# Rounds of maxima in twos on four PSUM banks, ahead of the main loop of a fused attention and MLP kernel

## The chip, the cores and the metric

The kernel runs on one core of a Trainium2 chip. The time is that of one execution on the device, in microseconds; three executions of the kernel before took 2324.1, 2325.55 and 2324.93 us, median 2324.93.

## The reference

For x of 2048 tokens by 576 channels the kernel computes `g * a + (1 - g) * b`:

```
g = sigmoid((x * gate_w).sum(-1))
a = softmax(q k^T * 18**-0.5) v, 32 heads of 18, then @ wo        (q, k, v = x @ wqkv)
b = gelu(layernorm(x) @ w1 + b1) @ w2 + b2                        (576 -> 4608 -> 576)
```

All of it is float32. The kernel splits each operand of a projection into a rounded high part and the rest, a low part, and multiplies high by high, high by low and low by high.

## The kernel before

**Two stages.** The first works through four blocks of 512 tokens (`tb` 0 to 3). For each block it transposes x on TensorE (`x_chunk`, five pieces, L711), copies the high parts with ScalarE and subtracts for the low parts with VectorE, and then does 17 groups (`g` 0 to 16): nine `qk_group`s (L784 to L787, 14 matmuls of 128 rows and 512 columns each, results copied and subtracted in L790 and L791, both stored to HBM) and eight `v_group`s (L805 to L808, 14 matmuls of 288 columns; copied by ScalarE in L812 or VectorE in L814, stored to `v_scr` after every second one). In between stand the layer norm of the block on VectorE (`norm`, L753 to L773), the transposes of the next block's x (after groups 2 to 6) and of the normed x (`y_chunk`, L735 and L736, stored to `y_scr`, after groups 8 to 12, in block 0 after 11 to 15).

The second stage is a loop of 512 steps: 32 units (a pair of heads by half of the queries), 16 blocks of keys each. It interleaves scores and exponentials of one unit (L250, L253), the weighted sum over v (L268), the maxima of the next unit (L210, L212) and, as filler of TensorE, the MLP (L460, L538).

**Rounds of maxima.** Softmax needs each row's maximum before the exponentials. A round (`s1_round`) is two matmuls of 54 rows, one for each head of the pair, in the upper and the lower half of the array (L210), into a PSUM bank each, and two VectorE reductions (L212). A unit has 32 rounds; the loop does two in a step. Since the loop starts with unit 0's exponentials, all 32 rounds of unit 0 and eight of unit 1 are done ahead of it. The table `ROUNDS` says after which groups of which block a round is put: one after each group from 8 on in block 1, from 2 on in block 2, from 5 on in block 3, 36 in all. The last four stand alone between the blocks and the loop (L1089, each with a call of `run_due`).

**PSUM.** Its eight banks in the first stage: four in the pool `ps_a` for the projections, three in `ps_s1` for all transposes and all rounds, and one in `ps_o`, which is first used by the loop. A pool's banks are handed out in turn, and the next user of a bank waits until the last one has been read. `score_bank` gives a round its banks.

**Order of the work.** Each engine does its instructions in the order in which the program writes them. SyncE's queue issues nearly all transfers, in order too, and an issue that waits for its data holds up those behind it. Small tasks are put at fixed places by `run_due`, which counts slots: one after each group of block 2 from group 4 on, one after each group of block 3 up to group 8 and two after each later one, then about four to a step of the loop. The first weights of the MLP are read ahead of the loop: `load_w1` and `load_w2` issue the reads of raw weights into buffers (one for w1, two for w2) and enter in `LOADED` the slot from which a `split` may use them: 5 and 3 slots later, in the loop 8 and 6. The split copies the high part with ScalarE (L370), subtracts on GpSimd (L166) and then lets the next raw piece be read into the buffer (L349, L355). Splits are first entered in block 3's group 9; a model of GpSimd's queue spreads them.

The weights of the first stage come in seven pieces (`W_CUT`); `split_w` copies the high part with ScalarE (L705) and subtracts on VectorE for pieces 0 and 1, on GpSimd for the others (L706). A group's matmuls wait for the pieces that they read.

Of the kernel before, what the change touches and what calls it, by code (L numbers as in the profile page):

```python
# [36 lines left out]
NS1 = 3  # L37
# [3 lines left out]
LAND = 8  # L41
# [5 lines left out]
LAST = 28  # L47
PSTEP = (489, 494, 497, 499)
ORDER = (0, 1, 3, 2)
ROUNDS = [lambda g: 0, lambda g: int(g >= 8), lambda g: int(g >= 2), lambda g: int(g >= 5)]  # L50
SLOTS = [lambda g: 0, lambda g: 0, lambda g: int(g >= 4), lambda g: 1 if g < 9 else 2]
SKIP = 0
N_AT = 5
# [7 lines left out]
def gated_mix_kernel(ctx: ExitStack, tc: tile.TileContext, x, wqkv, wo, w1, b1, w2, b2, gate_w, out):  # L61
    nc = tc.nc
# [32 lines left out]
    ps_s1 = ctx.enter_context(tc.tile_pool(name="ps_s1", bufs=NS1, space=PSUM))  # L95
    ps_o = ctx.enter_context(tc.tile_pool(name="ps_o", bufs=1, space=PSUM))
# [4 lines left out]
    def psum(pool):  # L101
        return pool.tile([P, TB], F32, name="ps")

    ring = [0]

    def score_bank():

        if not looped[0]:
            return psum(ps_s1)
        ring[0] += 1  # L110
        return psum(ps_s1 if ring[0] % (NS1 + 2) < NS1 else ps_s2)

    def big_tile():
# [5 lines left out]
    def bcast_rows(ap, n):  # L119
        return bass.AP(tensor=ap.tensor, offset=ap.offset, ap=[[0, P], [1, n]])  # L120
# [6 lines left out]
    slot = [0]  # L127
# [183 lines left out]
    looped = [False]  # L311

    def next_round():
        if rounds:
            u, r = rounds.pop()
            s1_round(u, r)
            if r == NR - 1:
                defer(1, lambda: s1_finish(u))


    def mlp():
# [3 lines left out]
        n = len(seq)  # L325
# [3 lines left out]
        def chunk(q):  # L329

            i, m = divmod(q, G // 2)
            return i, m, seq[i][1] * G + 2 * m
# [5 lines left out]
        LOADED = {}  # L338
        NQ0 = npair // NB

        def load_w1(q):

            if (1, q) in LOADED or q >= NQ0:
                return
            LOADED[1, q] = slot[0] + (LAND if looped[0] else 5)
            fc = chunk(q)[2]
            for h in range(2):
                src = w1[:, (fc + h) * P:(fc + h + 1) * P]
                nc.sync.dma_start(R1[64 * h:64 * h + 64], src.rearrange("(c p) n -> p c n", p=64))  # L349

        def load_w2(c):
            if (2, c) in LOADED or c >= NFC:
                return
            LOADED[2, c] = slot[0] + (LAND - 2 if looped[0] else 3)
            nc.sync.dma_start(R2[c % 2], w2[c * P:(c + 1) * P, :])  # L355

        def rounded(dst, src):
# [254 lines left out]
        for i in range(n + 1):  # L612
            q = 2 * i
# [49 lines left out]
    with ExitStack() as a:  # L663
        wpool = a.enter_context(tc.tile_pool(name="a_w", bufs=1, side="right"))
        sm = a.enter_context(tc.tile_pool(name="a_sm", bufs=2, side="right"))
        ps_a = a.enter_context(tc.tile_pool(name="ps_a", bufs=4, space=PSUM))
# [11 lines left out]
        def x_view(tb):  # L678
            return xt[tb].rearrange("p (t d) -> p t d", d=D + 64)
# [12 lines left out]
        def load_w(n):  # L692
            cs = slice(W_CUT[n], W_CUT[n + 1])
            wide = W_CUT[n + 1] - W_CUT[n]
            raw = pp.tile([P, 2, 2, TB], F32, name="p").rearrange("p a b c -> p (a b c)")[:, :5 * wide]
            raw = wraw[n] = raw.rearrange("p (c n) -> p c n", n=wide)
            nc.sync.dma_start(raw[:, 0:4, :], wqkv[0:512, cs].rearrange("(c p) n -> p c n", p=P))
            nc.sync.dma_start(raw[0:64, 4, :], wqkv[512:576, cs])
            nc.sync.dma_start(raw[64:128, 4, :], wqkv[512:576, cs])

        def split_w(n, eng):
            c0 = W_CUT[n] if W_CUT[n] < 2 * D else W_CUT[n] - 2 * D
            hi, lo = [w_[:, :, c0:c0 + W_CUT[n + 1] - W_CUT[n]] for w_ in (W_QK if W_CUT[n] < 2 * D else W_V)]
            raw = wraw.pop(n)
            nc.scalar.activation(hi, raw, AF.Copy)  # L705
            eng.tensor_tensor(lo, raw, hi.bitcast(F32), op=ALU.subtract)  # L706

        def transposed(tb, c):
            ps = psum(ps_s1)
            for t in range(4):  # L710
                nc.tensor.transpose(ps[:, t * P:(t + 1) * P], x_view(tb)[:, t, c * P:(c + 1) * P], ident)  # L711
            return ps
# [3 lines left out]
        def x_chunk(tb, c):  # L716

            if c == 0:
                xT[tb] = big_tile()
            big = xT[tb]  # L720
            ps = transposed(tb, c)
            if c < 4:
                nc.scalar.activation(big[:, c, :], ps, AF.Copy)
                nc.vector.tensor_tensor(big[:, 4 + c, :], ps, big[:, c, :].bitcast(F32), op=ALU.subtract)
            else:
                tmp = hp.tile([P, TB], F32R, name="hh")
                nc.scalar.activation(tmp, ps, AF.Copy)
                nc.scalar.activation(big[0:64, 8, :], ps[0:64], AF.Copy)
                nc.vector.tensor_tensor(big[64:128, 8, :], ps[64:128], tmp[64:128, :].bitcast(F32), op=ALU.subtract)

        def y_chunk(tb, c):
            ps = transposed(tb, c)
            eh = hp.tile([P, TB], F32R, name="hh")
            el = hp.tile([P, TB], F32R, name="hl")
            nc.scalar.activation(eh, ps, AF.Copy)  # L735
            nc.vector.tensor_tensor(el, ps, eh.bitcast(F32), op=ALU.subtract)  # L736
            for s_, e in enumerate((eh, el)):
                if c < 4:
                    nc.sync.dma_start(y_scr[tb, s_, 2 * c:2 * c + 2].rearrange("c p n -> (c p) n"), e.bitcast(F32))
                else:  # L740
                    nc.sync.dma_start(y_scr[tb, s_, 8], e[0:64].bitcast(F32))
# [94 lines left out]
        for tb in range(NB):  # L836
            work = [(qk_group, (tb, mt)) for mt in (range(9) if tb < 2 else (4, 0, 1, 2, 3, 5, 6, 7, 8))] + [(v_group, (tb, t, n)) for t in range(4) for n in range(2)]
            for g, (fn, args) in enumerate(work):
                if tb == 0:
                    if g in W_AT:  # L840
                        n = W_AT[g]
                        split_w(n, nc.gpsimd if n > 1 else nc.vector)
                        if n + 2 < 7:
                            load_w(n + 2)
                    if g == 10:
                        nc.sync.dma_start(b2b, bcast_rows(b2, D))
                        nc.sync.dma_start(b1r, b1.rearrange("(c p) -> c p", p=P))
                if tb == NB - 1 and g == 16:
                    args += (lambda: next(stream[0]),)
                fn(*args)  # L850
                ng = g - (N_AT if tb == 0 else 2)
                if 0 <= ng < 4:
                    norm(tb, ng)
                if tb + 1 < NB and 2 <= g < 7:
                    x_chunk(tb + 1, g - 2)
                yg = g - (11 if tb == 0 else 8)
                if 0 <= yg < 5:
                    y_chunk(tb, yg)
                if g == (16 if tb == 0 else 13) and tb + 2 < NB:
                    load_x(tb + 2)  # L860
                if tb == NB - 1:
                    if g == 1:
                        load_k(0, 3 * TB, S)
                    if g == 2:
                        load_q(1)
                        next(stream[0])
                    if g == 9:
                        qkstack.close()
                        wp1 = mstack.enter_context(tc.tile_pool(name="m_w1", bufs=3))
                        wp2 = mstack.enter_context(tc.tile_pool(name="m_w2", bufs=4))  # L870
                        next(stream[0])

                        nc.scalar.activation(gate, glog, AF.Exp, scale=-1.0)
                    if g == 14:
                        nc.vector.tensor_scalar(gate, gate, 1.0, None, op0=ALU.add)
                        nc.vector.reciprocal(gate, gate)
                        nc.vector.tensor_scalar(gate1, gate, -1.0, 1.0, op0=ALU.mult, op1=ALU.add)
                    if g == 7:
                        ps = psum(ps_s1)
                        nc.tensor.transpose(ps[:, :NFC], b1r, ident[:NFC, :NFC])  # L880
                        nc.vector.tensor_copy(b1t, ps[:, :NFC])
                if tb == 1 and g == 5:
                    load_q(0)
                    load_k(0, 0, TB)
                if tb == 1 and g == 9:
                    load_k(0, TB, 2 * TB)
                if tb == 2 and g == 4:
                    load_k(0, 2 * TB, 3 * TB)
                for _ in range(ROUNDS[tb](g)):
                    next_round()  # L890
                for _ in range(SLOTS[tb](g)):
                    run_due()
# [282 lines left out]
```

## Time and profile before

| | |
|---|---|
| median of three executions | 2324.93 us |
| profiled execution | 2325.55 us |
| its span, first to last instruction | 2323.8 us |
| mean granted TensorE clock | 0.996 |
| first loop matmul (L250) starts | 250.09 us into the span |
| rounds' reductions (L212), mean | 685 ns |

The span is one execution, recorded by the hardware profiler. In the lines below, a timeline row gives start and length in us, engine, line, operation, output and inputs, shapes, the number of instructions that were merged, and in brackets the idle time just before with what ended it. PE is TensorE's matmuls, PEld its weight loads, DVE is VectorE, ACT ScalarE, POOL GpSimd, SPq SyncE's queue. A matmul's length includes its way through the array, so the distance between starts tells the pace. Rows of stretches give the busy time of each engine, the granted clock and the DMA engines' mean share.

### The profile page before, as it was taken

The numbers are of one execution on the slowest core, as the hardware profiler recorded it, in microseconds if no ns is written. First come the engines' busy times: TensorE is split into PE (matmuls) and PEld (weight loads), VectorE is DVE, ScalarE is ACT, GpSimd is POOL, SyncE is SP. The second block draws the span as 40 slices with busy tenths as digits, with TensorE's granted clock in tenths as the row PEclk, the third lists the DMA queues.
The fourth block names the chain that finished last, engine by engine and source line by source line (L and its number), as shares of the span: only waits on it lengthen the run. The fifth ranks groups of instructions, "written<-read, shape, count | busy, mean of one in ns | idle before, by whom it ended". The sixth has DMA issues, their size and how long they took to land.

```text
span 2323.8 us, 51438 instructions
## 1 busy us (share of the span) xinstructions
PE 2292.7 (99%) x20585; PEld 1544.4 (66%) x20585; DVE 1664.8 (72%) x2890; ACT 1441.9 (62%) x2773; POOL 967.7 (42%) x965
## 2 busy tenths in 40 slices
PE   8998999999999999999999999999999999999999
PEld 7876666666666666666666666666666666666658
DVE  5665677777777777777777777777777777777734
ACT  4222577777776666666676666666666666666662
POOL 4001466666564433333353444444434333333700
PEclk9999899999999999999999999999999999999999
DMA  7747855444456524243263424242364233242264
GB/s 245 244 149 232 232 171 147 149 140 146 137 190 167 159 96 118 99 138 111 77 172 136 157 96 130 88 136 96 118 162 152 96 111 107 97 146 96 77 210 161
DMA packets 165022, 330.31 MB, mean 142 GB/s; under 512 B 57190, under 2 KB 84490, under 8 KB 154054
## 3 DMA queue, kind: packets, MB, share of 16 engines
q1 hardware_dynamic: 163162, 323.76, 44.3%
q8 instruction: 162, 2.65, 0.5%
q10 hardware_dynamic: 1620, 3.26, 0.4%
q14 instruction: 78, 0.64, 0.1%
HBM read 234.16 MB, written 96.58 MB: 142 GB/s over the span
## 4 chain that ended last, share of the span: by engine, by line
PE 92%; DVE 3%; DMA 2%; ACT 1%; issue 1%; SPq 1%; POOL 0%; ACTq 0%; DVEq 0%; POOLq 0%
PE ps L268 20%; PE ps L538 20%; PE ps L460 20%; PE ps L250 13%; PE ps L210 12%; PE ps L1071 3%; PE ps L784 3%; PE ps L805 2%; DVE m L212 1%; DMA qk_scr<-hh 1%; DMA p<-in_A_wqkv_dram 0%; PE ps L711 0%; ACT p L253 0%; DMA x<-in_B_w_dram 0%; DVE x L773 0%
## 5 line engine op out<-in xcount | busy, mean ns | idle before, releaser
L212 DVE TENSOR_REDUCE m<-ps 128x1 f32<-128x512 f32 x2048 | 1314.8, 685 | 393.7 <-PE ps L210 372.2
L253 ACT ACTIVATE p<-ps 128x512 f32<-128x512 f32 x1368 | 740.6, 594 | 372.2 <-PE ps L250 361.9
L166 POOL TENSOR_SCALAR zz<-zz 128x512 f32<-128x512 f32 x288 | 178.6, 620 | 819.1 <-ACT zz L513 802.9
L460 PE MATMUL ps<-big,w 64*128 64x512 f32 x3888 | 510.4, 393 | 0.1
L253 ACT ACTIVATE ring<-ps 128x512 f32<-128x512 f32 x680 | 368.2, 594 | 187.6 <-PE ps L250 182.9
L538 PE MATMUL ps<-w,hh 64*128 64x288 f32 x4352 | 466.3, 299 | 4.0 <-ACT token L547 3.5
L210 PE MATMUL ps<-ka,qa 54*128 54x512 f32 x2048 | 457.9, 422 | 11.0 <-DVE hl L736 6.5
L250 PE MATMUL ps<-qa,ka 56*128 56x512 f32 x2048 | 454.7, 423 | 0.7 <-DVE m L212 0.4
L460 PEld LDWEIGHTS ps<-big,w 64*128 64x128 f32 x3888 | 371.4, 185 | 82.3 <-ACT z L481 0.4
L538 PEld LDWEIGHTS ps<-w,hh 64*128 64x128 f32 x4352 | 370.7, 186 | 45.5 <-ACT token L547 17.3
L166 POOL TENSOR_TENSOR zz<-zz,z 128x512 f32<-128x512 f32 x288 | 371.7, 1291 | 24.0
L250 PEld LDWEIGHTS ps<-qa,ka 56*128 56x128 f32 x2048 | 204.3, 184 | 216.6 <-DVE m L212 180.8
L268 PE MATMUL ps<-p,vt 128*32 128x512 f32 x2736 | 345.0, 599 | 0.0
L538 PE MATMUL ps<-w,hl 64*128 64x288 f32 x2176 | 333.8, 293 | 0.0
L210 PEld LDWEIGHTS ps<-ka,qa 54*128 54x128 f32 x2048 | 206.6, 186 | 110.6 <-ACT p L253 42.4
L166 POOL TENSOR_TENSOR w<-x,w 128x576 fp32r<-128x576 f32 (+1 forms) x54 | 98.3, 1836 | 307.2 <-DMA qk_scr<-hh 172.2
L538 PEld LDWEIGHTS ps<-w,hl 64*128 64x128 f32 x2176 | 215.5, 185 | 0.3 <-POOL hl L166 0.3
L166 POOL TENSOR_TENSOR hl<-zz,hh 128x512 fp32r<-128x512 f32 x136 | 176.6, 1299 | 11.3
L268 PE MATMUL ps<-ring,vt 128*32 128x512 f32 x1360 | 179.1, 598 | 0.0
L268 PEld LDWEIGHTS ps<-p,vt 128*32 128x32 f32 x2736 | 71.5, 109 | 161.2 <-issue 153.9
L556 DVE SCALAR_TENSOR_TENSOR x<-ps,x 128x288 f32<-128x288 f32 x256 | 105.1, 452 | 57.3 <-PE ps L538 57.3
L784 PE MATMUL ps<-big,wqk 128*128 128x512 f32 x432 | 109.7, 402 | 1.5 <-POOL wqk L706 1.4
(101 smaller groups left out, 1394.0 us busy)
## 6 DMA issues: line engine op xcount, KB each, us to landing
w<-w_scr SPq DMA_DIRECT2D x54, 1152.0 KB
w<-w_scr SPq DMA_DIRECT2D x108, 576.0 KB
x<-in_B_w_dram SPq DMA_DIRECT2D x72, 288.0 KB
w_scr<-w SPq DMA_DIRECT2D x18, 1152.0 KB
w_scr<-w SPq DMA_DIRECT2D x36, 576.0 KB
big<-y_scr SPq DMA_DIRECT2D x42, 384.0 KB
qa<-qk_scr SPq DMA_DIRECT2D x192, 72.0 KB
ka<-qk_scr SPq DMA_DIRECT2D x84, 144.0 KB
```

The lines of the kernel that those rows point to most:

```text
L166: fn(*args, **kw)
L210: nc.tensor.matmul(ps, qa[r0:r0 + 54, t * P:(t + 1) * P], ka[r0:r0 + 54, kb * TB:(kb + 1) * TB], start=True, stop=True)
L212: nc.vector.tensor_reduce(M4[u][:, h, t, kb:kb + 1], ps, axis=AX.X, op=ALU.max)
L250: nc.tensor.matmul(ps[h], ka[r0:r0 + 56, kc * P:(kc + 1) * P], qa[r0:r0 + 56, qb * TB:(qb + 1) * TB], start=True, stop=True)
L253: nc.scalar.activation(RING[n % 3][:, qb, h], ps[h], AF.Exp, scale=SCALE)
L268: nc.tensor.matmul(OB[u][r:r + 32, :], v[:, k, 19 * h:19 * h + 32], RING[c % 3][:, qb, h, :], start=(k == 0), stop=(k == NT - 1))
L460: nc.tensor.matmul(ps[h], wt[w_][r, c, :], Y[s_][r, c, :], start=(k == 0), stop=(k == 26))
L538: mm = nc.tensor.matmul(ps[nn][:, :ND], h_[r, tok], w_[p_][r, cs[nn]], start=(k == 0), stop=(k == 6 * G - 1))
L556: nc.vector.scalar_tensor_tensor(dst, ps[nn][:, :ND], 0.5, b2b[:, cs[nn]] if g == 0 else dst, op0=ALU.mult, op1=ALU.add)
L784: nc.tensor.matmul(ps, w_[:, c, ms], big[:, s_, :], start=(k == 0), stop=False)
L805: nc.tensor.matmul(ps[:, :ND], big[:, s_, tok], w_[:, c, cs], start=(k == 0), stop=False)
L1071: nc.tensor.matmul(ps[:, :ND], OT[b][2][:, s_, tok], w_part(w_, c)[:, cs], start=(k == 0), stop=(k == 13))
```

## The change

Transposes take their banks from the projections' pool, and rounds go around four banks (the three of `ps_s1` and `ps_o`). Rounds stand in twos: four pairs in block 1 (after groups 9, 11, 13, 15), eight in block 2 (after the odd groups to 15) and eight in block 3 (after 6, 8, 10, 12, 13, 14, 15, 16), 40 rounds in all, so that none is left for the place between the blocks and the loop, nor its four calls of `run_due`. Raw weights are used from the eighth slot after their read is issued, ahead of the loop as well. Piece 2 of the first stage's weights is subtracted on VectorE.

```diff
-ROUNDS = [lambda g: 0, lambda g: int(g >= 8), lambda g: int(g >= 2), lambda g: int(g >= 5)]
+ROUNDS = [lambda g: 0, lambda g: 2 * (g in (9, 11, 13, 15)), lambda g: 2 * (g % 2 and g != 17),
+          lambda g: 2 * (g in (6, 8, 10, 12, 13, 14, 15, 16))]
...
     def score_bank():
 
+        ring[0] += 1
         if not looped[0]:
-            return psum(ps_s1)
-        ring[0] += 1
+            return psum(ps_s1 if ring[0] % (NS1 + 1) < NS1 else ps_o)
         return psum(ps_s1 if ring[0] % (NS1 + 2) < NS1 else ps_s2)
...
-            LOADED[1, q] = slot[0] + (LAND if looped[0] else 5)
+            LOADED[1, q] = slot[0] + LAND
...
-            LOADED[2, c] = slot[0] + (LAND - 2 if looped[0] else 3)
+            LOADED[2, c] = slot[0] + (LAND - 2 if looped[0] else LAND)
...
         def transposed(tb, c):
-            ps = psum(ps_s1)
+            ps = psum(ps_a)
...
-                        split_w(n, nc.gpsimd if n > 1 else nc.vector)
+                        split_w(n, nc.gpsimd if n > 2 else nc.vector)
...
                     if g == 7:
-                        ps = psum(ps_s1)
+                        ps = psum(ps_a)
                         nc.tensor.transpose(ps[:, :NFC], b1r, ident[:NFC, :NFC])
```

## The prediction

> **What bounds the kernel now.** I read the page's busy shares first, then the chain of waits, then busy time by stretch, and last each engine's timeline around the places that the diff names.
>
> ```profile
> PE 2292.7 (99%) x20585; PEld 1544.4 (66%) x20585; DVE 1664.8 (72%) x2890; ACT 1441.9 (62%) x2773; POOL 967.7 (42%) x965
> ```
>
> TensorE bounds the whole: 99% of the span is matmul time, and this change alters no matmul except where it stands. So the gain can only come from the stretch ahead of the main loop, which the diff rearranges, and most of its gaps lie at its end:
>
> ```profile
> 156.00:196.00 40.00, 40.00 (x224) 32.93 (x223) 24.17 (x49) 8.09 (x16) 0.00 (x0) 1.00 0.53 182
> 196.00:220.00 24.00, 22.23 (x108) 16.24 (x107) 16.43 (x33) 7.84 (x13) 1.21 (x1) 1.00 1.07 276
> 220.00:236.00 16.00, 9.18 (x54) 7.06 (x52) 6.62 (x14) 3.52 (x7) 7.02 (x5) 0.89 0.81 274
> 236.00:248.00 12.00, 10.94 (x54) 8.48 (x54) 8.46 (x18) 2.91 (x4) 3.38 (x2) 0.86 0.55 163
> 248.00:262.00 14.00, 13.69 (x78) 11.42 (x77) 8.45 (x15) 4.54 (x9) 1.89 (x1) 0.76 1.11 252
> ```
>
> The columns are length, PE, PEld, DVE, ACT, POOL, granted clock, DMA share, GB/s. From 220 to 236 PE has 9.2 us of work in 16, and the clock is below 1 until 262. But look at the DMA share: about 1.1 at both ends of this table, so two resources are near their limit there. DMA has slack only in the middle: 16 x (1.07 - 0.81) + 12 x (1.07 - 0.55) = **10.4 us**.
>
> The gap itself, and the end of the stage:
>
> ```profile
> 229.35 0.68 ACT L370 ACTIVATE w<-x 128x576 fp32r<-128x576 f32 x1 [6.76 <-DMA x<-in_B_w_dram]
> 232.31 0.68 ACT L370 ACTIVATE w<-x 128x576 fp32r<-128x576 f32 x1 [2.28 <-DMA x<-in_B_w_dram]
> 232.90 0.58 ACT L735 ACTIVATE hh<-ps 128x512 fp32r<-128x512 f32 x1
> 234.25 1.39 PE L210 MATMUL ps<-ka,qa 54*128 54x512 f32 x2 [6.46 <-DVE hl L736]
> 245.91 4.31 PE L210 MATMUL ps<-ka,qa 54*128 54x512 f32 x7 [0.55 <-DVE m L212]
> 250.09 1.39 PE L250 MATMUL ps<-qa,ka 56*128 56x512 f32 x2
> ```
>
> ACT reads raw weights (L370) that have not landed; queued behind these reads is the copy L735 of the last transposed block, DVE's subtraction behind that, and a round of maxima (L210) that wants its bank. PE stands 6.46 us. Then four rounds alone (x7 and one more) run at DVE's pace before the loop's first matmul at 250.09.
>
> ```profile
> 245.26 0.33 SPq L815 DMA_DIRECT2D v_scr<-vt  x1
> 249.66 0.55 SPq L196 DMA_DIRECT2D vt<-v_scr  x1
> 262.29 0.16 PEld L268 LDWEIGHTS ps<-p,vt 128*32 128x32 f32 x8 [0.36 <-DMA vt<-v_scr]
> ```
>
> And this decides the tail: the loop's first weighted sum over v, at 262.29, waits 0.36 us for v read back from HBM, whose store SP issued at 245.26. The four lone rounds and the half clock lie beside that transfer. Taking them out of PE alone gains 0.36 us; the rest depends on how much earlier the store and the loads around it are issued.
>
> **Part by part.**
>
> *Third weight piece (n = 2) split on DVE instead of POOL.*
>
> ```profile
> 12.17 1.66 DVE L706 TENSOR_TENSOR wqk<-p,wqk 128x1440 fp32r<-128x1440 f32 x1 [0.60 <-ACT wqk L705]
> 17.60 1.41 ACT L705 ACTIVATE wqk<-p 128x1440 fp32r<-128x1440 f32 x1 [3.45 <-DMA p<-in_A_wqkv_dram]
> 19.14 6.57 POOL L706 TENSOR_TENSOR wqk<-p,wqk 128x1440 fp32r<-128x1440 f32 x2 [8.08 <-ACT wqk L705]
> 22.49 2.60 PE L784 MATMUL ps<-big,wqk 128*128 128x512 f32 x10 [1.36 <-POOL wqk L706]
> ```
>
> POOL takes 6.57 / 2 = 3.3 us, DVE 1.66 for the same shape. From ACT's end at 19.0 DVE is done at 20.7, ahead of the PE start at 21.1 that now slips to 22.49. Behind it on DVE stands the subtraction of one projection, which nobody awaits within a microsecond. Gain **1.36**; what is late next is the fifth and later pieces, which shift with it. Bounds 0 to 1.36.
>
> *Rounds in twos.* One round among 128-row matmuls, against a pair of 64-row matmuls that follows another:
>
> ```profile
> 48.50 1.74 PE L805 MATMUL ps<-wv,big 128*128 128x288 f32 x12
> 50.35 0.49 PE L711 MATMUL ps<-ident,x 128*128 128x128 f32 x3
> 109.46 1.87 PE L805 MATMUL ps<-wv,big 128*128 128x288 f32 x12
> 111.96 1.85 PE L805 MATMUL ps<-wv,big 128*128 128x288 f32 x12
> 256.53 0.47 PE L250 MATMUL ps<-qa,ka 56*128 56x512 f32 x2
> 256.76 0.47 PE L210 MATMUL ps<-ka,qa 54*128 54x512 f32 x2
> 256.99 2.34 PE L460 MATMUL ps<-big,w 64*128 64x512 f32 x18
> ```
>
> A v group alone repeats after 50.35 - 48.50 = 1.85 us, with a round after 111.96 - 109.46 = 2.50: the round costs 0.64. In the loop, where everything around has 64 rows, two matmuls cost 256.76 - 256.53 = 0.23. So 0.4 of the 0.64 is the change of shape, paid once for two rounds: a pair costs 0.64 + 0.23 = 0.87 (taken, as the second round follows a 64-row pair as in the loop) and at most 1.28. In blocks 1 and 2, 24 single rounds become 12 pairs: 24 x 0.64 - 12 x 0.87 = **4.9**; bounds 0 and 4.9.
>
> *Banks.* In block 2 transposes and rounds share three banks while DVE is busy with the norms:
>
> ```profile
> 126.82 0.60 PE L711 MATMUL ps<-ident,x 128*128 128x128 f32 x4
> 127.78 3.06 PE L784 MATMUL ps<-big,wqk 128*128 128x512 f32 x12
> 131.15 0.60 PE L711 MATMUL ps<-ident,x 128*128 128x128 f32 x4
> 136.66 0.66 PE L711 MATMUL ps<-ident,x 128*128 128x128 f32 x4 [0.65 <-DVE big L724]
> 146.74 0.66 PE L711 MATMUL ps<-ident,x 128*128 128x128 f32 x4
> 148.35 3.06 PE L784 MATMUL ps<-big,wqk 128*128 128x512 f32 x12
> ```
>
> An undisturbed group takes 131.15 - 126.82 = 4.33. The four groups from 126.82 to 146.74 take 19.92 instead of 17.32 (2.60 lost), and the last transposes to the next projection 1.61 instead of 0.96 (0.65 lost): **3.25**. Afterwards four transposes-or-projections and two rounds can be open, so PE may run two groups (over 8 us) ahead of DVE. Adding up DVE's work by group (a round is two reductions of 0.64, from the 1314.8 us for 2048 quoted below), I find it at most about 4 us behind. Gain 3.25, bounds 0 and 3.25.
>
> ```profile
> L212 DVE TENSOR_REDUCE m<-ps 128x1 f32<-128x512 f32 x2048 | 1314.8, 685 | 393.7 <-PE ps L210 372.2
> ```
>
> So block 3 starts 1.36 + 4.9 + 3.25 = **9.5 us** earlier. DMA does not forbid it: its share is 0.53 until 196.
>
> *Block 3 and the loop's head.* The first three raw reads don't move: their splits are entered at slot 23, after their old due slots (18 and 20) and at the new ones. The next reads of w2 move from slots 27 and 28 to 32 and 33, that is two projections later, behind the copy L735, and transposes no longer hold up rounds. So the 6.46 us go. How soon could PE alone reach the loop?
>
> ```profile
> 178.18 3.06 PE L784 MATMUL ps<-big,wqk 128*128 128x512 f32 x12
> ```
>
> Block 3 and the lone rounds last from 178.18 to 250.09, 71.9 us. Its work is 9 projections at 4.33 - 0.64 = 3.69 (that counts four transposed blocks too many, which pays for the two small transposes of bias and maxima), 8 v groups at 1.85 and 8 pairs at 0.87: 33.2 + 14.8 + 7.0 = 55 us, and about 1 for DVE, which has four pairs in the last four groups. That would be 16 us sooner relative to block 3's start. What is late next:
>
> ```profile
> 213.47 0.60 ACT L735 ACTIVATE hh<-ps 128x512 fp32r<-128x512 f32 x1 [1.50 <-DMA qk_scr<-hh]
> 236.81 1.15 ACT L370 ACTIVATE w<-x 128x1152 fp32r<-128x1152 f32 x1
> 238.03 2.66 POOL L166 TENSOR_TENSOR w<-x,w 128x1152 fp32r<-128x1152 f32 x1 [3.56 <-ACT w L370]
> 240.72 1.39 SPq L349 DMA_DIRECT2D x<-in_B_w_dram  x2
> ```
>
> At 213.47 ACT already waits for stores behind the 1.07 of DMA, so it stays there. From there the raw pieces still land near 228 and 231 (229.35 and 232.31, a microsecond sooner, as the reads ahead of them stand behind fewer stalls); the second w1 piece, now at slot 35, is copied after them (0.7 and 0.4 for ACT's v copy, then 1.15), split on POOL (2.66), and only then may SP reload its buffer (1.39), with the store of v queued behind. 231.3 + 0.7 + 0.4 + 1.15 + 2.66 + 1.39 gives about 238, and 239 to 240 with the waits between the queues. That is 5 to 7 us before 245.26: I take **6**, between 0 and the slack of 10.4. PE then waits at the loop's head for y and v, which costs clock: the three stretches lost 16 x 0.11 + 12 x 0.14 + 14 x 0.24 = 6.8 us of full clock, much of it hidden. A low window after the v transfer would be unhidden; I take **2**, bounds 0 and 3.4 (the last stretch's loss).
>
> The Trainium skill, TensorE: Matmul & The Clock Gate, Part 1, says that the clock halves after an idle window of about 3.4 us and recovers after a busy one; by it the new wait at the loop's head is a price of this change. The trace agrees for the 6.46 us stall, but its low clock at 248 to 262 follows a stretch where PE was busy 10.94 of 12 us, so here sparse work is enough. By the page the sum would lose one such window.
>
> *Sum.* 9.5 + 6 - 2 = 13.5 us. The profiled execution took 2325.55 us for a span of 2323.8, and is the slowest of the three shown (median 2324.93), so 0.6 lies between; 2325.55 - 13.5 gives the forecast of **2312 us**, against the median 2311.4. The loop's four slots fewer before its start delay the third w1 piece to the loop's second step; beside the wait for y and v that costs nothing, and about 1.2 (its ACT copy) if that wait is not there.
>
> **The rivals.**
> 1. *DMA does not hold the head*: y and v arrive as soon as PE does. Then 9.5 + 16 = 25 us, 2300. Against it: a share of 1.11 and the 0.36 wait. 0.12.
> 2. *The stall only moves*: ACT's v copies or the later raw reads wait for DMA as long as before, the store stays at 245.26 less the shift. 9.5 less 2 for the clock, 2317 to 2318. For it: 1.07. With pairs that cost 1.28 instead of 0.87 the shift is 4.6, and 2321. Together 0.20.
> 3. *Transposes wait for projections' banks.* If DVE falls over 8 us behind, twice what I count, each of the 35 transposed blocks in blocks 0 to 2 pays a wait like the 0.65 at 136.66: 35 x 0.65 = 23 us lost against 13.5, 2335. For it: DVE's runs of two rounds last 2.6 us. 0.07.
> 4. *The change doesn't do what it says*: rounds in twos just wait for reductions, the banks were no limit, and the later reads meet the same landing; within 4 us, near 2324. 0.07.
>
> **The numbers.** The forecast (2306 to 2316) has 0.54. The range 2300 to 2321 takes in rival 2 and half of rival 1 and leaves out rivals 3 and 4: 0.54 + 0.20 + 0.06 = 0.80. A measurement of this kernel can tell about 0.2% (4.7 us) from no change. Faster by more: 0.54 + 0.12 + most of rival 2 (0.18) = 0.84; within: 0.09; slower: 0.07.
>
> **What would show it.** PE's gap by POOL at 22.49 gone; a pair of rounds at about 0.87; no DVE wait between 126 and 149; block 3's first projection at 169 instead of 178; no 6 us gap behind L735; and instead PE waiting at the loop's head for `big<-y_scr` or `vt<-v_scr`, with low clock there. Wrong would be a DVE wait ahead of L711, or a loop head without DMA waits.

## The result, and the profile after

The changed kernel took 2315.3 us (median of six executions, 2312.5 to 2316.53) where the kernel before took 2325.63 (six on the same chip, 2324.1 to 2326.21): ratio 0.9955, 95% interval 0.9942 to 0.9968. That is 10.3 us less by the medians. The profiled execution, 2316.53 us, is the slowest of its six; its span is 2314.7, 9.1 us shorter than before's.

First the busy shares of the changed kernel's page, then its busy time by the stretches that the prediction shows of before (length, PE, PEld, DVE, ACT, POOL, granted clock, DMA share, GB/s):

```profile
PE 2286.9 (99%) x20585; PEld 1539.2 (66%) x20585; DVE 1665.4 (72%) x2891; ACT 1441.6 (62%) x2773; POOL 964.6 (42%) x964
```

```profile
156.00:196.00 40.00, 40.00 (x213) 32.79 (x212) 26.22 (x60) 6.80 (x14) 0.00 (x0) 1.00 0.64 188
196.00:220.00 24.00, 22.99 (x126) 18.19 (x124) 14.50 (x28) 8.50 (x14) 5.43 (x3) 0.93 1.01 306
220.00:236.00 16.00, 13.80 (x76) 9.76 (x78) 14.48 (x27) 5.58 (x10) 5.47 (x3) 0.94 0.73 237
236.00:248.00 12.00, 8.33 (x48) 5.35 (x44) 2.58 (x4) 3.22 (x5) 2.61 (x1) 0.78 1.12 215
248.00:262.00 14.00, 13.30 (x89) 8.04 (x91) 5.81 (x9) 6.99 (x13) 8.61 (x10) 0.77 0.86 201
```

PE's hole has moved. Before it lay at 220 to 236 (9.18 busy of 16); now that stretch has 13.80, and 236 to 248 has 8.33 of 12 at a DMA share of 1.12. Before, TensorE waited there for VectorE's subtraction behind the raw weights; now it waits, later, for y.

The places that the prediction named, in the timeline of TensorE. Lines of the changed kernel are one higher than before's:

```profile
20.44 3.04 PE L785 MATMUL ps<-big,wqk 128*128 128x512 f32 x12
...
106.71 1.86 PE L806 MATMUL ps<-wv,big 128*128 128x288 f32 x12
...
111.28 1.86 PE L806 MATMUL ps<-wv,big 128*128 128x288 f32 x12
...
144.22 1.87 PE L211 MATMUL ps<-ka,qa 54*128 54x512 f32 x4
...
169.85 2.96 PE L785 MATMUL ps<-big,wqk 128*128 128x512 f32 x12
```

The twelve matmuls at 20.44 are unbroken: the gap by POOL is gone, and block 1 starts 1.59 us earlier (61.20 instead of 62.79). Between 106.71 and 111.28 lie two v groups and one pair: 4.57 - 2 x 1.85 = 0.87 us for the pair, as forecast. At 144.22 a pair takes 1.87 instead of 0.73; that is the one wait left in blocks 1 and 2. Block 3 starts at 169.85, before at 178.18.

The reason for the 1.87, from VectorE's timeline:

```profile
143.06 2.48 DVE L213 TENSOR_REDUCE m<-ps 128x1 f32<-128x512 f32 x4
```

These are the reductions of the pair issued at 136.39, delayed by the norm. The next pair, two groups of matmuls later, needs the same four banks.

Then the loop's head, TensorE first, SyncE's queue next, one row of the chain of waits, and the row of the DMA view that gives the size of these reads:

```profile
231.12 0.56 PE L251 MATMUL ps<-qa,ka 56*128 56x512 f32 x2 [0.55 <-DVE m L213]
...
241.74 0.49 PE L461 MATMUL ps<-big,w 64*128 64x512 f32 x1 [0.34 <-DMA big<-y_scr]
244.69 1.65 PE L461 MATMUL ps<-big,w 64*128 64x512 f32 x5 [2.46 <-DMA big<-y_scr]
246.50 0.79 PE L461 MATMUL ps<-big,w 64*128 64x512 f32 x1 [0.16 <-DMA big<-y_scr]
248.70 1.64 PE L461 MATMUL ps<-big,w 64*128 64x512 f32 x5 [1.41 <-DMA big<-y_scr]
...
251.12 3.56 PE L269 MATMUL ps<-p,vt 128*32 128x512 f32 x16
251.12 0.20 PEld L269 LDWEIGHTS ps<-p,vt 128*32 128x32 f32 x8 [0.65 <-DMA vt<-v_scr]
```

```profile
230.01 1.37 SPq L350 DMA_DIRECT2D x<-in_B_w_dram  x2
231.47 0.58 SPq L816 DMA_DIRECT2D v_scr<-vt  x1
232.14 4.05 SPq L125 DMA_DIRECT2D big<-y_scr  x6
236.46 0.38 SPq L197 DMA_DIRECT2D vt<-v_scr  x1
```

```profile
235.59 13.07 DMA big<-y_scr
```

```profile
big<-y_scr SPq DMA_DIRECT2D x6, 384.0 KB
```

TensorE reaches the loop's first scores at 231.12, 19 us earlier than before (250.09). But the first weighted sum over v comes at 251.12, only 11.2 earlier (262.29). In between it waits four times, 4.4 us in all, for the low part of y, the six reads of 384 KB that SP issues from 232.14 on. The last of them holds the chain for 13.07 us, and the first weighted sum over v then takes 3.56 us at half clock. The last row of the first fence is that sum's weight load: v came last for it, in a gap of 0.65 us. That is also the ordinary gap between weight loads at half clock (0.66 later in the same sum), so v comes just in time and holds TensorE hardly or not at all.

### The profile page after: what moved, and what is told of

The parts are those of the page before. It is cut to its first block, busy times and chain, and to the rows that moved or that the text cites. A ratio compares the mean times of both kernels' runs of the same rounds, so it can differ in the third digit from the quotient of the medians.

```text
span 2314.7 us, 51444 instructions
## 1 busy us (share of the span) xinstructions
PE 2286.9 (99%) x20585; PEld 1539.2 (66%) x20585; DVE 1665.4 (72%) x2891; ACT 1441.6 (62%) x2773; POOL 964.6 (42%) x964
## 4 chain that ended last, share of the span: by engine, by line
PE 93%; DVE 3%; DMA 1%; issue 1%; ACT 1%; SPq 1%; POOL 0%; ACTq 0%; DVEq 0%; POOLq 0%
PE ps L269 20%; PE ps L539 20%; PE ps L461 19%; PE ps L251 13%; PE ps L211 12%; PE ps L785 4%; PE ps L1072 3%; PE ps L806 2%; DVE m L213 1%; DMA big<-y_scr 1%; PE ps L712 0%; ACT p L254 0%; PE ps L788 0%; PE ps L787 0%; DVE x L774 0%
## 5 line engine op out<-in xcount | busy, mean ns | idle before, releaser
L211 PE MATMUL ps<-ka,qa 54*128 54x512 f32 x2048 | 450.7, 420 | 3.2 <-DVE m L213 1.4
```

Of the source, the lines that this page charges most:

```text
L211: nc.tensor.matmul(ps, qa[r0:r0 + 54, t * P:(t + 1) * P], ka[r0:r0 + 54, kb * TB:(kb + 1) * TB], start=True, stop=True)
```

## The experiments

Each kernel is the changed one with the edit shown, except where it says otherwise. Times of events are us into the span of the profiled execution; ratios are against the kernel before on the same chip. There is no number 8.

| kernel | median us | ratio, 95% interval | block 3 | first scores | first sum over v | span |
|---|---|---|---|---|---|---|
| before | 2325.63 | | 178.18 | 250.09 | 262.29 | 2323.8 |
| changed | 2315.3 | 0.9955 (0.9942 to 0.9968) | 169.85 | 231.12 | 251.12 | 2314.7 |
| 1 piece 2 on POOL | 2314.61 (one) | | 171.23 | 230.93 | 251.46 | 2312.8 |
| 2 raw reads as before | 2321.27 | 0.9980 (0.9970 to 0.9989) | 171.25 | 240.43 | 258.04 | 2321.0 |
| 3 single rounds | 2319.17 | 0.9968 (0.9955 to 0.9980) | 173.48 | 233.78 | 254.45 | 2317.4 |
| 4 old banks | 2362.24 | 1.0156 (1.0141 to 1.0171) | 201.95 | 277.42 | 297.20 | 2359.8 |
| 5 last four rounds alone | 2316.84 | 0.9959 (0.9946 to 0.9971) | 169.91 | 231.28 | 250.91 | 2312.1 |
| 6 third w1 piece behind y | 2322.77 | 0.9986 (0.9978 to 0.9995) | 170.03 | 229.55 | 246.93 | 2319.7 |
| 7 other places in block 2 | 2317.55 | 0.9967 (0.9955 to 0.9978) | 169.98 | 232.55 | 251.21 | 2313.7 |
| 9 before, late raw reads | 2324.94 | 0.9995 (0.9986 to 1.0004) | 178.32 | 242.18 | 260.44 | 2324.6 |
| 10 as 6, user in time | 2313.96 | 0.9957 (0.9943 to 0.9971) | 169.83 | 230.64 | 247.29 | 2310.6 |
| 11 y's low part not read | 2306.94 | 0.9923 (0.9910 to 0.9937) | 169.91 | 231.31 | 243.37 | 2304.8 |
| 12 as 10, with 5 | 2313.24 | 0.9944 (0.9932 to 0.9957) | 170.00 | 231.28 | 245.01 | 2310.9 |
| 13 changed, again | 2317.79 | 0.9961 (0.9947 to 0.9974) | 169.95 | 231.21 | 251.54 | 2316.0 |

### 1. The third weight piece

```diff
-                        split_w(n, nc.gpsimd if n > 2 else nc.vector)
+                        split_w(n, nc.gpsimd if n > 1 else nc.vector)
```

> The changed kernel with weight piece 2 subtracted on GpSimd again. My theory: the 1.36 us wait of TensorE near 21 us returns, block 1's first projection starts 1.6 us later than in the changed kernel (62.8 instead of 61.20 us into the span), and all that follows shifts with it, as the transfers of block 3 are issued later too: about 2317 to 2318 us. Rival: the head of the loop waits for transfers anyway and swallows the shift: first weighted sum over v still near 251.1, time as the changed kernel's 2315.

TensorE's wait is back:

```profile
22.25 2.60 PE L785 MATMUL ps<-big,wqk 128*128 128x512 f32 x10 [1.17 <-POOL wqk L707]
```

Block 3 starts 1.38 us later, and the first sum over v 0.34 later. Nothing of it is seen at the end (one execution, with a mean granted clock of 0.996 against 0.995). So in this execution the part's 1.4 us is real where it arises and absorbed at the loop's head.

### 2. The raw weights' slots

```diff
-            LOADED[1, q] = slot[0] + LAND
+            LOADED[1, q] = slot[0] + (LAND if looped[0] else 5)
...
-            LOADED[2, c] = slot[0] + (LAND - 2 if looped[0] else LAND)
+            LOADED[2, c] = slot[0] + (LAND - 2 if looped[0] else 3)
```

> The changed kernel with raw weights used 5 and 3 slots after their read is issued, as before. My theory: ScalarE stands at the raw w2 pieces ahead of the last transposed block's copy again; rounds have banks of their own now, but their reductions stand behind that block's subtraction on VectorE, so TensorE waits 4 to 5 us one pair of rounds later than before; block 3 ends about 4 us later and the y transfer with it: 2 to 5 us slower than the changed kernel (2317 to 2320). Rival: the separate banks alone removed the 6.46 us gap: no wait over 1.5 us in block 3, time within 1 us of the changed kernel.

ScalarE's reads of raw weights wait for their transfers (first fence), and TensorE stands behind them, by way of VectorE (second):

```profile
220.13 0.68 ACT L371 ACTIVATE w<-x 128x576 fp32r<-128x576 f32 x1 [6.41 <-DMA x<-in_B_w_dram]
```

```profile
226.09 2.58 PE L211 MATMUL ps<-ka,qa 54*128 54x512 f32 x4 [7.98 <-DVE m L213]
```

The first scores come 9.3 us later, the first sum over v 6.9, the median ratio goes from 0.9955 to 0.9980. But 1.4 us of this stands already at block 3 (171.25 instead of 169.85), before any raw weight is used; 0.82 of it is a wait of TensorE for x at 72.37 in this execution, which the edit doesn't touch. So with pairs and banks in place the later slots are worth 5.5 us at the first sum over v, and 6 by the medians. The wait of 7.98 us is longer than the 4 to 5 expected, and the time a little above the range.

### 3. Single rounds, on the four banks

`ROUNDS` as before.

> The changed kernel with the old table of rounds: 36 single ones in the blocks, four alone ahead of the loop; new banks, later raw reads and piece 2 on VectorE stay. My theory: 24 single rounds at 0.64 us instead of 12 pairs at 0.87 us cost 4.9 us in blocks 1 and 2, less the 1.2 us for which a pair now waits near 144: block 3's first projection at 173.5 to 175 instead of 169.85, and a time 3 to 5 us above the changed kernel's (2318 to 2320). Rival: twos bring nothing by themselves, the banks did it all: block 3 starts at 169 to 171, within 1 us of the changed kernel or faster.

Block 3 starts at 173.48 instead of 169.85, 3.63 us later. That is the pairs' worth in blocks 1 and 2, and it agrees with the prices: 24 x 0.64 - 12 x 0.87 = 4.92, less the 1.2 us that the pair at 144.22 waits. 3.3 of it arrive at the first sum over v. The run also prices the banks alone: with single rounds and new banks block 3 starts 178.18 - 173.48 = 4.70 us sooner than before the change, less 1.59 for piece 2 that is 3.11, against the forecast's 3.25.

### 4. Pairs, on the old banks

```diff
-            return psum(ps_s1 if ring[0] % (NS1 + 1) < NS1 else ps_o)
+            return psum(ps_s1)
...
-            ps = psum(ps_a)
+            ps = psum(ps_s1)
```

(The last edit stands at two places.)

> The changed kernel with transposes and rounds back on the three banks of ps_s1; twos, later raw reads and piece 2 on VectorE stay. My theory: a pair needs four banks and has three, and transposes queue for them behind the reductions, so TensorE waits 1 to 2 us for VectorE at most of the 20 pairs: 15 to 30 us slower than the changed kernel, 5 to 20 slower than the kernel before (2330 to 2345). Rival: banks hardly matter, the shape switches do: within 3 us of the changed kernel.

The direction is as expected, the size is not: the span is 45.1 us longer than the changed kernel's (2359.8 against 2314.7), where 2330 to 2345, 15 to 30 more than the changed kernel's median, had been expected. Two rows of TensorE, and its busy time in two stretches, show what that sum left out:

```profile
142.45 1.39 PE L211 MATMUL ps<-ka,qa 54*128 54x512 f32 x2 [4.47 <-DVE big L725]
143.77 5.49 PE L785 MATMUL ps<-big,wqk 128*128 128x512 f32 x12
```

```profile
138.00:144.00 6.00, 1.55 (x3) 0.80 (x4) 5.49 (x17) 0.69 (x2) 0.00 (x0) 0.86 0.24 87
144.00:149.00 5.00, 5.00 (x12) 3.90 (x13) 0.79 (x2) 0.00 (x0) 0.00 (x0) 0.50 0.00 0
```

A pair needs four banks where three are shared with transposes, so its second round waits for VectorE (4.47 us), and then TensorE runs at 0.50 of its clock: the next twelve matmuls take 5.49 instead of 3.0. The waits themselves are as expected: between 60 and 270 us TensorE waits 26.2 us for VectorE ahead of rounds, in 18 places. Long ones are paid again in clock: summed over stretches of 20 us, the granted clock lost is worth 27 us of full speed here and 12 in the changed kernel (an estimate, since some of it lies where TensorE idles).

### 5. The last four rounds alone

```diff
-          lambda g: 2 * (g in (6, 8, 10, 12, 13, 14, 15, 16))]
+          lambda g: 2 * (g in (6, 8, 10, 12, 13, 14))]
```

> The changed kernel with the last four rounds (the pairs after groups 15 and 16 of block 3) standing alone between the blocks and the loop again, as before the change. My theory: they are free there, since the loop's first weighted sum over v waits for the y and v transfers, which are issued when the last v group is done; that group comes about 1.7 us sooner without two pairs ahead of it: first weighted sum at 249.5 to 251, time from 0 to 2 us below the changed kernel's 2315. Rival: lone rounds run at VectorE's pace and cost the path their 5.5 us, less 1.7: 3 to 4 us above the changed kernel.

The last matmul of the last v group starts at 227.40 instead of 229.62, but SyncE's queue is no earlier:

```profile
230.11 1.38 SPq L350 DMA_DIRECT2D x<-in_B_w_dram  x2
231.58 0.58 SPq L816 DMA_DIRECT2D v_scr<-vt  x1
232.25 4.04 SPq L125 DMA_DIRECT2D big<-y_scr  x6
```

What SyncE's queue waited for between 224 and 240, in the view of waits (us in total, times, longest):

```profile
SPq L350 <- POOL w L167: 4.7, 1, 4.7
```

It stands at the read of the third w1 piece (L350) until POOL has split the second, and the store of v and the reads of y come behind it. The first sum over v is at 250.91 instead of 251.12. Whether these four rounds stand in groups or alone is worth nothing here: they lie under the queue's wait and y's transfer.

### 6. The third w1 piece read behind y

```diff
-                defer(3 if looped[0] else 1 if raw != (1, 2) else 6, lambda: then(raw[1]))
+                defer(3 if looped[0] else 1 if raw not in ((1, 1), (1, 2)) else 6, lambda: then(raw[1]))
```

> The changed kernel with the read of the third raw w1 piece (two issues, 0.6 MB) issued five slots later, so that it stands behind the y and v reads on SyncE's queue. My theory: SyncE no longer stands at 225 to 230 for GpSimd's subtraction, y is issued about 1 us sooner and does not share the DMA engines with that piece; TensorE's waits for y (4.4 us in four places) shrink by 2 to 4 us and the low clock with them: 2 to 4 us below the changed kernel (2311 to 2313). Rival: the y read is bound by its own 2.4 MB and by the buffer that the last v group frees, or the later piece makes its user wait: within 1 us of the changed kernel or slower.

SyncE issues the store of v at 228.91 instead of 231.47, and the first sum over v comes at 246.93, 4.2 us sooner. Then:

```profile
264.72 0.50 PE L461 MATMUL ps<-big,w 64*128 64x512 f32 x2 [3.13 <-ACT w L371]
267.41 2.50 PE L461 MATMUL ps<-big,w 64*128 64x512 f32 x10 [2.19 <-POOL w L167]
```

The piece is copied and split too late, since its copy is due eight slots after the read and the planner's estimate of POOL's queue holds it back further (experiment 10 alters both), and TensorE waits 5.3 us for it. The profiled span is 5 us longer than the changed kernel's: in time the rival's outcome, though the head does what the theory said.

### 7. Other places for block 2's pairs

Block 2's pairs stand after groups 0, 1, 6, 7, 9, 11, 13 and 15.

> The changed kernel with block 2's pairs after groups 0, 1, 6, 7, 9, 11, 13, 15 instead of the odd ones to 15, so that none stands among the norms (groups 2 to 5). My theory: the wait at 144.2, where four matmuls take 1.87 instead of 0.73 us because the reductions of the pair two groups earlier come only then, is gone: block 3's first projection at 168.6 to 168.8 instead of 169.85, and about 1.2 us off the time (2314). Rival: the wait moves to another pair, block 3's start stays within 0.3 us.

```profile
144.46 1.77 PE L211 MATMUL ps<-ka,qa 54*128 54x512 f32 x4
...
251.21 3.64 PE L269 MATMUL ps<-p,vt 128*32 128x512 f32 x16 [0.34 <-DMA vt<-v_scr]
```

The pair after group 7 still waits, now for the reductions of the pair after group 6, which come at 143.19, and it costs nearly the same; block 3 starts at 169.98. The rival was right. The second row shows v itself late: in this execution TensorE waits 0.34 us for it.

### 9. The kernel before, with the later raw reads alone

The two lines of experiment 2 the other way round, in the kernel before.

> The kernel before with only the later use of raw weights (8 slots after the read). My theory: the 6.46 us gap ahead of the round at 234.25 goes or shrinks below 3 us, but the weighted sum over v waits for y and v, whose reads are issued some 4 to 6 us sooner: 2 to 5 us below the kernel before (2321 to 2324). Rival: the gap's full 6.5 us comes off (2319). Second rival: the wait only moves, and the time is within 1 us of the kernel before.

The 6.46 us gap is gone, and the loop's first scores come at 242.18, 7.9 us sooner. SyncE's queue and TensorE behind it:

```profile
240.78 0.58 SPq L815 DMA_DIRECT2D v_scr<-vt  x1
241.45 4.07 SPq L124 DMA_DIRECT2D big<-y_scr  x6
```

```profile
254.13 2.49 PE L460 MATMUL ps<-big,w 64*128 64x512 f32 x6 [1.93 <-DMA big<-y_scr]
258.01 1.65 PE L460 MATMUL ps<-big,w 64*128 64x512 f32 x5 [1.39 <-DMA big<-y_scr]
260.44 3.62 PE L268 MATMUL ps<-p,vt 128*32 128x512 f32 x13
```

The store of v is issued at 240.78 instead of 245.26, 4.5 us sooner; the first sum over v comes 1.85 sooner and then runs at half clock (13 of its matmuls in 3.62 us). The time doesn't move, as the second rival had it. Taking the largest gap of TensorE out by itself is worth nothing; the transfer takes its place.

### 10. As 6, with the piece's user in time

```diff
-            LOADED[1, q] = slot[0] + LAND
+            LOADED[1, q] = slot[0] + (6 if q == 2 else LAND)
...
-            queue = raw[0] ** 2 * SLOT
+            queue = 8 * SLOT if raw == (1, 2) else raw[0] ** 2 * SLOT
```

(with the line of experiment 6)

> The changed kernel with the third w1 piece read behind y, as in the version whose gain was given back, but with the user of that piece no longer late: its ACT copy is due 6 slots after the read instead of 8, and the estimate of POOL's queue that held it back is raised from one slot to eight for this piece alone. Theory (the head waits for the low part of y, and that version lost its 4.2 us only because the piece was split after 264): the first weighted sum over v stays near 247 instead of 251.1, the piece is split on POOL before 256, PE doesn't wait ahead of it, and the end comes 3 to 5 us before the changed kernel's, near 2311. Rival (whatever is read behind y comes too late, since DMA is full until 256): the first weighted sum over v near 247, but a new wait ahead of the third w1 piece or of the scores' next rows, and 2315 or more.

```profile
243.30 0.50 PE L461 MATMUL ps<-big,w 64*128 64x512 f32 x1 [1.87 <-DMA big<-y_scr]
245.30 1.21 PE L461 MATMUL ps<-big,w 64*128 64x512 f32 x5 [1.50 <-DMA big<-y_scr]
247.29 2.87 PE L269 MATMUL ps<-p,vt 128*32 128x512 f32 x16
```

Both late waits of experiment 6 are gone and the profiled span is 4.1 us shorter than the changed kernel's, as the theory has it. But the five executions spread from 2311.8 to 2316.9, the profiled one has a mean granted clock of 0.998 against the changed kernel's 0.995, and the ratio, 0.9957, is the changed kernel's; the median, 2313.96, lies between the theory's 2311 and the rival's 2315. So the mechanism is shown in the trace, its worth at the end is not.

### 11. The head without the read of y's low part

The loop's first block multiplies the high part of y twice; the six reads are left out.

```diff
+            if tb == 0 and s_ == 1:
+                Y[1] = Y[0]
+                return
-            if s_ not in Y:
+            if s_ not in Y or (tb == 1 and s_ == 1 and c0 == 0):
                 Y[s_] = big_tile()
...
+            held = dict(Y)
...
-                    nc.tensor.matmul(ps[h], wt[w_][r, c, :], Y[s_][r, c, :], start=(k == 0), stop=(k == 26))
+                    nc.tensor.matmul(ps[h], wt[w_][r, c, :], held[s_][r, c, :], start=(k == 0), stop=(k == 26))
```

> The changed kernel without the first read of y's low part: the loop's first block multiplies the high part in its place (so that part of the sum is left out in effect), the number of matmuls is the same, and 2.3 MB are not read at the loop's head. Theory (the loop's head waits for this read alone): the four waits of 4.4 us for big<-y_scr are gone, with them the low clock behind them, and the first weighted sum over v comes near 245 instead of 251.1; 4 to 6 us less, 2309 to 2311. Rival (v, which is read back behind y in any case, is as late): the first weighted sum over v waits for vt<-v_scr and comes at 249 or later; 2313 or more.

```profile
243.37 1.92 PE L269 MATMUL ps<-p,vt 128*32 128x512 f32 x16
```

No wait for DMA is left at the head, v is there in time, the clock is full (1.92 us for the sixteen matmuls that took 3.56), and the first sum over v comes 7.75 us sooner. The median is 8.4 us below the changed kernel's (7.4 by the two ratios), more than the 4 to 6 expected. The clock counts as well: the fifth sum over v comes 9.4 us sooner, 1.6 of it from the first sum at full clock. So that read holds the head, and it does so twice over: TensorE waits for it, and v stands behind it in SyncE's queue, landing just in time in the changed kernel and here with time to spare.

### 12 and 13. The piece behind y and four lone rounds, beside the changed kernel

Experiment 6's line, experiment 10's second, and experiment 5's; and the changed kernel again on the same chip.

> The changed kernel with the third w1 piece read behind y and its user in time (estimate of POOL's queue raised for this piece), and in addition the last two pairs of rounds taken out of block 3's v groups and run alone behind them, so that the last v group, which holds y's buffer, ends some 2 us sooner. Theory (the head waits for the low part of y, whose read can start when the last v group ends and SP is free): the store of v and the reads of y are issued at about 228 instead of 230, the first weighted sum over v comes near 245.5 instead of 247.3, and the end 5 to 6 us before the changed kernel's, 2309 to 2311. Rival (behind the head DMA is full in any case, so what the head gains is given back in the next 20 us, as about 1.5 us of 3.8 were before): the first weighted sum over v near 245.5, but 2312 to 2315, not to be told from the changed kernel.

> The changed kernel itself, unaltered, on the same chip as the version beside it, so that the two can be compared there. Every theory expects what it gave before: a ratio to the kernel before of 0.9942 to 0.9968, 2312 to 2318.

SyncE, TensorE and ScalarE of kernel 12:

```profile
228.24 0.33 SPq L816 DMA_DIRECT2D v_scr<-vt  x1
228.66 3.95 SPq L125 DMA_DIRECT2D big<-y_scr  x6
```

```profile
243.44 0.96 PE L461 MATMUL ps<-big,w 64*128 64x512 f32 x5 [1.28 <-DMA big<-y_scr]
245.01 1.92 PE L269 MATMUL ps<-p,vt 128*32 128x512 f32 x16
249.47 0.49 PE L251 MATMUL ps<-qa,ka 56*128 56x512 f32 x1 [2.11 <-ACT ring L254]
```

```profile
247.77 1.16 ACT L371 ACTIVATE w<-x 128x1152 fp32r<-128x1152 f32 x1 [2.87 <-DMA x<-in_B_w_dram]
```

With SyncE's queue free, the earlier end of the last v group counts: y is issued 3.5 us sooner than in the changed kernel, and the first sum over v comes 6.1 sooner, at full clock. About 2 us are given back at 249.47, where the exponentials stand behind a raw piece that has not landed, and more in half clock behind that wait: by the second sum over v 3.3 us of the lead are left (259.41 instead of 262.75). On this chip the median is 4.5 us below the changed kernel's (2313.24 against 2317.79). The intervals of the two ratios overlap a little, so that it is the better version is likely and not certain. The theory expected 2309 to 2311; the time lies in the rival's 2312 to 2315, and the rival's reason, that the head's gain is given back behind it, is what the trace shows.

## Why the prediction was right, and where its sum was off

The forecast was 2312 and the measurement 2315.3: the bound, the direction and the order of the stages held. The size was partly luck: by the two profiles the change brought 9.1 us and not 13.5, and 2315.3 is nearer to the 2317 to 2318 of rival 2 than to 2312. The traces, not the time, tell these two apart. The forecast's own sum of 13.5 us, against the two profiled executions (9.1):

| term | predicted | measured | from |
|---|---|---|---|
| piece 2 | 1.36 | 1.59 | block 1 at 61.20 instead of 62.79 |
| rounds in twos, and banks | 8.15 | 6.74 | block 3 8.33 sooner, less 1.59 |
| block 3 and the loop's head | 6 | 2.84 | first sum over v 11.17 sooner, less 8.33 |
| clock at the head | -2 | -2.1, a remainder | span 9.1 shorter, less 11.17 |

*Piece 2*: right in block 0. Experiment 1 adds that the head takes most of it back, 1.38 at block 3 and 0.34 at the first sum over v, so that the term should be worth little at the end.

*Rounds in twos*: the price of a pair, 0.87, was right to the digit, and experiment 3 shows the term by itself (3.63, with the one wait in it, against 4.9) and the banks beside it (3.11 against 3.25).

*Banks*: here the step that VectorE is at most about 4 us behind, so that nothing waits, failed at one place, the pair at 144.22, for 1.2 us: the reductions of the pair at 136.39 began about 6 us after its matmuls were done (143.06). The step counted VectorE's work group by group and asked whether it falls two groups behind; it did not ask whether the four banks of one pair are read before the next pair, and at the norm's end they are not. The predicted sign of a wrong step, a wait ahead of the transposes (L712), is not there: transposes do not wait for projections' banks. Rival 3 is out. Experiment 4 shows what the banks are worth together with twos: without them twos are slower than the kernel before.

*Block 3 and the head*: this is the term that was mis-sized, 6 predicted and 2.84 measured. Its first half was right: the store of v was issued at 231.47 instead of 245.26, that is 13.79 sooner, of which 8.33 is the shift of block 3, and 5.46 remain, in the predicted 5 to 7. What failed is the step behind it, that the first sum over v follows the store. Before, it came 17.0 us after the store; now 19.7. The prediction named y and v together as what TensorE would wait for, but sized only the store of v. What holds the head is the read of y's low part (experiment 11), with the third w1 piece ahead of it in the queue (experiments 6, 10 and 12): 2 x 288 KB before 6 x 384. Before the change, that w1 piece had been issued 4.5 us ahead of the store of v, and TensorE came to its first MLP matmul 7.5 us after the store (252.76) instead of 2.1 (233.52).

All the runs agree on this. Where the third w1 piece is issued 1.5 to 2.1 us ahead of the store of v (changed, 1, 3, 4, 5, 7, 9 and 13), the first sum over v starts 19.3 to 20.0 us after the store; where it is issued 4.5 us or more ahead, or behind v (before, 2, 6, 10 and 12), 16.8 to 18.3; and 11.7 where y's low part is not read (experiment 11). The reads of q that SyncE issues right behind v don't explain it: experiment 9 has none there and takes 19.7, experiment 2 has them and takes 18.3.

One reading behind this step was also too strong. The 0.36 us that the prediction took for a wait for v is the ordinary gap between weight loads at full clock (the second sum, at 272.28, shows 0.36 with no transfer named), and TensorE's matmuls show no wait there. Before the change v landed just in time; it did not yet hold the head.

*Clock*: the price was right, as far as a remainder shows it. The 3.56 us of the first sum over v, where 1.92 is full clock, are 1.6 of it; the same sum takes 3.51 in experiment 13 and 2.52 in experiment 1, so the size varies between runs.

*Rivals*: rival 1 (the head is free) is wrong by experiment 11's difference. Rival 2 (the stall only moves) is right for the later raw reads taken alone (experiment 9: nothing gained), and wrong for the whole. The parts don't add: raw slots alone 0.0005 of the time, all but the raw slots 0.0020, everything 0.0045. By these ratios 0.0020 come only with both together, with an interval of about 0.001 on each side of every ratio. Rival 4 is out.

Open stays how much of kernel 12's gain is real at the end. Executions of one kernel spread over 4 to 7 us here, and the quicker ones have the higher granted clock (experiment 9: 2319.43 us at 0.998, 2326.42 at 0.995). Some half-clock stretches worth about 1.8 us each, near 1680 and 2220 us, are in some profiles and not in others (experiment 7 lacks the first, experiment 5 the second). So 2 us between two profiled spans mean little; why the clock differs, no run tells.

## What to carry to other kernels

When a gap of the bounding engine is about to go, look for the transfer that lay under it, and size that transfer with all that stands ahead of it in the same queue; only what arrives sooner at the next point that needs data is gained. Pair small work of another shape so that the change of shape is paid once, but give each pair its own banks, and check that the reader of one pair is done before the next, at the place where that reader has most else to do. A read that is moved behind the urgent one must have its user moved along, or the gain is given back.

## What the runs showed of the hardware that was not expected

The granted clock of TensorE falls to half also without one long gap. Three stretches of the changed kernel:

```profile
232.00:244.00 12.00, 9.47 (x56) 6.68 (x56) 5.83 (x10) 5.10 (x9) 1.48 (x1) 0.86 1.07 244
244.00:249.00 5.00, 2.74 (x8) 1.42 (x10) 0.00 (x0) 0.00 (x0) 1.12 (x1) 0.52 1.12 195
249.00:254.00 5.00, 5.00 (x25) 1.78 (x23) 1.95 (x3) 2.69 (x5) 1.69 (x2) 0.50 0.58 167
```

The longest wait there is 2.46 us, and the clock stays at 0.50 for five us of unbroken work behind it. The same half clock followed the single wait of 4.47 us in experiment 4. The Trainium skill, TensorE: Matmul & The Clock Gate, Part 1, ties the half clock in its table of states to an idle window of about 3.4 us. Experiment 4 agrees with it, and the changed kernel does not need so long a wait. So in this kernel waits of 1 to 2.5 us close together were paid twice, once as waits and once as clock. Shorter ones can be too: from 234 to 237 us the clock is 0.50 as well, behind waits of 0.55 and 0.47 us (at 231.12 and 232.32). Yet in experiment 1 waits of 0.55 and 0.46 at the same place are followed by full clock from 232 to 240, and what decides between the two is open.
